# Loading four adjacent heads in one 128-partition DMA, with gated queues and a rewritten opening, in a fused attention and MoE kernel

## The chip, the cores and the metric

The kernel runs on one core of one Trainium2 chip. The metric is the device time of one execution in microseconds, taken as the median over runs. The engines are named as in the profile: PE (TensorE matmul), PEld (TensorE weight load), DVE (VectorE), ACT (ScalarE), POOL (GpSimd) and SP (SyncE, which here only issues DMAs).

## The reference

A ReLU-squared attention without softmax, followed by a two-layer feed-forward block with a quick GELU. All inputs and the output are float32.

```python
q, k, v: (8, 12, 448, 64)          # batch, heads, sequence, head size
scores = (1/sqrt(64)) * q @ k^T
attn   = max(scores, 0)**2 / 448
x      = (attn @ v) as (3584 tokens, 768)
h      = x @ w_in                  # (768, 2048)
g      = h * sigmoid(1.702 * h)
out    = g @ w_out                 # (2048, 768)
```

## The kernel before

The attention is cut into 24 units (`NU`), three for each of the 8 batches. A unit holds four heads: partitions 0 to 63 carry one pair of heads and partitions 64 to 127 another. A token is written as p*7 + j, so each partition p holds 7 tokens and the attention of a unit runs in 7 slots j.

For each unit, `load` (L66) issues six DMAs on SP, two halves of 64 partitions for each of k, q and v, in float32. `cast` (L79) turns k and q into float16 on DVE and v on POOL. `trans` (L91) issues two transposing DMAs on SP, which give kT and qT with the head size on the partitions. One slot is then `scores` (L99: four 64x64x448 matmuls into the PSUM tile sc), `relu2` (L113: ReLU on ACT from PSUM into rl, then rl*rl on DVE into at) and `av_mm` (L120: four matmuls that accumulate over the 7 slots of the unit in the PSUM tile av). `xt_evac` (L135) copies av as float16 into xt, the transposed input of the feed-forward part.

The feed-forward part works on 8 blocks of 384 or 512 tokens in turn (`gblk`). `m1(g, f)` (L175) makes one of 16 slices of the hidden layer: six matmuls into ht, GELU on ACT into gf, and a scaling to float16 on POOL into gt. `m2(g, m, h)` (L195) makes 128 tokens by 384 columns of the output: 16 matmuls into op, a scaling on DVE into osb and, behind the second half, two output DMAs on SP.

Every engine runs its instructions in the order in which the program emits them. `visit(n)` (L155) emits the scores of the next n slots, the av matmuls of the slots visited last, and the ReLU and multiply of the new slots. The opening loads and prepares units 0 to 2, then issues w1 (four casting DMAs for w_in) on POOL, loads units 3 to 5 and issues w2 (four casting DMAs for w_out), and only then emits the first visits. After the first batch the list `moe` interleaves m1 of block g with m2 of block g-1, and a visit of two slots is emitted whenever the estimated matmul time since the last one passes `TV = 3.4`. `step_visit` first calls `prefetch(u + 4, u + 2)`, which loads up to unit u+3 and prepares unit u+1.

The pools that matter: three buffers for each staged tensor, two for the float16 casts, four for v16, three for kT and qT, three for rl, six for at, three for xt and gf, three for osb; PSUM has two buffers for sc, one for av and two that ht and op share.

Of the kernel before, what the change touches and what calls it, by code (L numbers as in the profile page):

```python
# [6 lines left out]

F32 = mybir.dt.float32
F16 = mybir.dt.float16
AF = mybir.ActivationFunctionType  # L10
# [4 lines left out]
def kernel(  # L15
# [9 lines left out]
    nc = tc.nc  # L25
# [8 lines left out]
    NOUT = DM // 2  # L34
    SC = float(D * S)
    WQ = 4


    gblk = [6, 8] * (B // 2)
# [12 lines left out]
    xtp = ctx.enter_context(tc.tile_pool(name="xtp", bufs=3))  # L52
    gfp = ctx.enter_context(tc.tile_pool(name="gfp", bufs=3))
    gtp = ctx.enter_context(tc.tile_pool(name="gtp", bufs=2))
    osp = ctx.enter_context(tc.tile_pool(name="osp", bufs=3))
    ps_s = ctx.enter_context(tc.tile_pool(name="ps_s", bufs=2, space=bass.MemoryType.PSUM))
    ps_v = ctx.enter_context(tc.tile_pool(name="ps_v", bufs=1, space=bass.MemoryType.PSUM))
    ps_m = ctx.enter_context(tc.tile_pool(name="ps_m", bufs=2, space=bass.MemoryType.PSUM))

    win = [cst.tile([128, NK, WQ * 128], F16, name=f"win{i}") for i in range(NF // WQ)]  # L60
    wout = [cst.tile([128, WQ, DM], F16, name=f"wout{i}") for i in range(NF // WQ)]


    units = {}

    def load(u):  # L66
        b, pr = divmod(u, NP)
        st = {}
        for n, t in (("k", k), ("q", q), ("v", v)):
            x = stp.tile([128, 2, S], F32, name=f"{n}st", tag=f"{n}st")  # L70
            for s in range(2):
                h0 = 6 * s + 2 * pr
                nc.sync.dma_start(  # L73
                    out=x[64 * s:64 * s + 64, :, :],
                    in_=t[b, h0:h0 + 2].rearrange("a (p j) d -> p a (j d)", j=J))
            st[n] = x
        units[u] = st

    def cast(u):  # L79
        st = units[u]  # L80
        for n in ("k", "q"):
            c = c16.tile([128, J, 2, D], F16, name=f"{n}16", tag=f"{n}16")
            nc.vector.tensor_copy(  # L83
                out=c.rearrange("p j a d -> p a j d"),
                in_=st[n].rearrange("p a (j d) -> p a j d", d=D))
            st[n + "16"] = c
        vv = v16p.tile([128, 2, J, D], F16, name="v16", tag="v16")
        nc.gpsimd.tensor_copy(out=vv, in_=st["v"].rearrange("p a (j d) -> p a j d", d=D))  # L88
        st["v16"] = vv

    def trans(u):  # L91
        st = units[u]
        for n in ("k", "q"):
            t = qkT.tile([128, J, 128], F16, name=f"{n}T", tag=f"{n}T")
            nc.sync.dma_start_transpose(  # L95
                out=t[:, :, :], in_=st[n + "16"].rearrange("p j a d -> p (j a d)"))
            st[n + "T"] = t

    def scores(u, j):  # L99
        st = units[u]  # L100
# [11 lines left out]

    def relu2(u, j, sc):  # L113
        rl = rlp.tile([128, 2, S], F16, name="rl", tag="rl")
        nc.scalar.activation(out=rl, in_=sc[:, :, 0:S], func=AF.Relu)  # L115
        at = atp.tile([128, 2, S], F16, name="at", tag="at")
        nc.vector.tensor_tensor(out=at, in0=rl, in1=rl, op=ALU.mult)  # L117
        return at

    def av_mm(u, j, at):  # L120
        st = units[u]
        if j == 0:
            st["av"] = ps_v.tile([128, 2, 512], F32, name="av", tag="av")
        for s in range(2):
            for a in range(2):
                r = slice(64 * s, 64 * s + 64)
                nc.tensor.matmul(  # L127
                    out=st["av"][64 * a:64 * a + 64, s, 0:S],
                    lhsT=st["v16"][r, a, j, :],
                    rhs=at[r, a, :],  # L130
                    start=(j == 0), stop=(j == J - 1))

# [42 lines left out]
    def m1(g, f):  # L175
        n = 64 * gblk[g]
        if f == 0:
            gts[g] = gtp.tile([128, NF, 512], F16, name="gt", tag="gt")
        ht = ps_m.tile([128, 512], F32, name="ht", tag="mm")
        w = win[f // WQ]  # L180
        fo = (f % WQ) * 128
        for kk in range(NK):
            nc.tensor.matmul(  # L183
                out=ht[:, 0:n], lhsT=w[:, kk, fo:fo + 128],
                rhs=xts[g][:, kk // NP, kk % NP, 0:n],
                start=(kk == 0), stop=(kk == NK - 1))
        gf = gfp.tile([128, 512], F32, name="gf", tag="gf")
        nc.scalar.activation(out=gf[:, 0:n], in_=ht[:, 0:n],  # L188
                             func=AF.Gelu_apprx_sigmoid, scale=1.0 / SC)
        nc.gpsimd.tensor_scalar(out=gts[g][:, f, 0:n], in0=gf[:, 0:n],  # L190
                                scalar1=SC, scalar2=1.0, op0=ALU.mult, op1=ALU.mult)
# [3 lines left out]
    def m2(g, m, h):  # L195
        if h == 0:
            osb[g, m] = osp.tile([128, DM], F32, name="osb", tag="osb")
        ot = osb[g, m]
        op = ps_m.tile([128, 512], F32, name="op", tag="mm")
        for f in range(NF):  # L200
            nc.tensor.matmul(  # L201
                out=op[:, 0:NOUT],
                lhsT=gts[g][:, f, m * 128:(m + 1) * 128],
                rhs=wout[f // WQ][:, f % WQ, h * NOUT:(h + 1) * NOUT],
                start=(f == 0), stop=(f == NF - 1))
        nc.vector.tensor_scalar(out=ot[:, h * NOUT:(h + 1) * NOUT], in0=op[:, 0:NOUT],  # L206
                                scalar1=1.0 / SC, scalar2=None, op0=ALU.mult)
        if h == 1:
            for i in range(2):
                b, j = divmod(gcum[g] + 2 * m + i, J)  # L210
                r0 = b * S + j
                nc.sync.dma_start(out=out[r0:r0 + 63 * J + 1:J, :],
                                  in_=ot[64 * i:64 * i + 64, :])

    def w1(i):
        nc.gpsimd.dma_start(  # L216
            out=win[i],
            in_=moe_w_in[:, i * WQ * 128:(i + 1) * WQ * 128].rearrange(
                "(kk p) f -> p kk f", p=128))

    def w2(i):
        nc.gpsimd.dma_start(  # L222
            out=wout[i],
            in_=moe_w_out[i * WQ * 128:(i + 1) * WQ * 128, :].rearrange(
                "(f p) d -> p f d", p=128))


    moe = []

    def t1(g):  # L230
        return 6 * (64 * gblk[g] / 2400.0 + 0.0025)

    T2 = 16 * (NOUT / 2400.0 + 0.0025)
    for ph in range(1, NG + 2):
        a = [("m1", ph - 1, f) for f in range(NF)] if ph - 1 < NG else []
        c = ([("m2", ph - 2, m, h) for m in range(gblk[ph - 2] // 2) for h in range(2)]
             if ph >= 2 else [])
        if a and c:
            seq = []
            ci = 0  # L240
            for i, x in enumerate(a):
                seq.append(x)
                while ci < len(c) and (i + 1) * len(c) >= (ci + 1) * len(a):
                    seq.append(c[ci])
                    ci += 1
            seq += c[ci:]
        else:
            seq = a + c
        moe += seq

    with tc.manual_schedule():
        loaded = [0]
        prepped = [0]

        def prefetch(upto_load, upto_prep):
            while loaded[0] < min(NU, upto_load):
                load(loaded[0])
                loaded[0] += 1
            while prepped[0] < min(NU, upto_prep):
                cast(prepped[0])  # L260
                trans(prepped[0])
                prepped[0] += 1

        prefetch(2, 0)
        prefetch(2, 1)
        prefetch(3, 2)
        prefetch(3, 3)
        for i in range(NF // WQ):
            w1(i)
        prefetch(6, 3)  # L270
        for i in range(NF // WQ):
            w2(i)

        def step_visit(n):
            u = slots[pos[0]][0]
            prefetch(u + 4, u + 2)
            visit(n)


        while done_units[0] < NP:  # L280
            if pos[0] < NP * J:
                step_visit(min(2, NP * J - pos[0]))
            else:
                visit(0)
        acc = 0.0
        TV = 3.4
        m1_done = 0
        for it in moe:
            if it[0] == "m1":
                g = it[1]  # L290
                need = NP * min(B, -(-gcum[g + 1] // J))
                while done_units[0] < need:
                    if pos[0] < len(slots):
                        step_visit(2)
                    else:
                        visit(0)
                m1(*it[1:])
                acc += t1(g)
            else:
                m2(*it[1:])  # L300
                acc += T2
            if it[0] == "m1" and it[2] == NF - 1:
                m1_done = it[1] + 1
            if acc >= TV and (pos[0] < len(slots) or pend):

                if pos[0] < len(slots):
                    if slots[min(pos[0] + 1, len(slots) - 1)][0] // NP + 1 - 3 < m1_done:
                        step_visit(2)
                else:
                    visit(0)  # L310
                acc -= TV


# [28 lines left out]
```

## Time and profile before

| What | us |
|---|---|
| median of three runs | 461.97 |
| lowest and highest | 460.99 and 463.29 |
| the profiled execution | 461.49 |
| its span, first to last instruction | 459.7 |
| PE busy | 391.4 |
| ACT busy | 212.0 |
| DVE busy | 192.6 |
| POOL busy | 107.4 |

The profile gives one execution. Busy time of PE includes matmuls that run at half clock: the line PEclk says in tenths which part of the full clock was granted in each slice. The DMA share is the mean busy share of the 16 DMA engines of the core, and the GB/s count the bytes as written, so that a casting DMA from float32 to float16 counts half of what it reads. In lists of waits the columns are the time in all, how often, and the longest one. In lists in order of time they are start, duration, engine, line, operation, operands and, in brackets, the idle time before it and what ended that.

### The profile page before, as it was taken

How to read it: one execution, taken by the hardware profiler on the slowest of the kernel's cores; microseconds unless marked ns; L12 is line 12 of the kernel's file. 1: busy time of each engine (PE TensorE's matmuls, PEld its weight loads, DVE VectorE, ACT ScalarE, POOL GpSimd, SP SyncE). 2: the span in 40 equal slices, each digit the busy share in tenths (PEclk: the TensorE clock that was granted, in tenths of full speed). 3: DMA queues.
4: the chain of work that ended last, by engine and by line, in shares of the span. 5: the costliest groups of instructions: out<-in, count | busy, mean ns of one | idle time of the engine just before them, and what ended most of it. 6: DMA issues, size and time to landing. Idle time of an engine off the chain costs nothing.

```text
span 459.7 us, 7621 instructions
## 1 busy us (share of the span) xinstructions
PE 391.4 (85%) x3008; PEld 196.2 (43%) x3008; DVE 192.6 (42%) x308; ACT 212.0 (46%) x298; POOL 107.4 (23%) x164
## 2 busy tenths in 40 slices
PE   0276208878999899989998999989999999999995
PEld 0032104333444455544444555534444555455563
DVE  1387002575653445565444355356364634200021
ACT  1295105775664355466553545456564545322200
POOL 0060202501231222223142133213222212122200
PEclk9997757959999999999999999999999999999999
DMA  8999999799462589539831888198093311111132
GB/s 191 229 223 272 233 202 230 156 209 230 93 145 51 148 149 208 116 91 224 194 80 41 156 193 194 36 210 179 2 187 83 68 44 36 34 26 28 34 88 68
DMA packets 75044, 61.84 MB, mean 135 GB/s; under 512 B 47872, under 2 KB 71424, under 8 KB 75008
## 3 DMA queue, kind: packets, MB, share of 16 engines
q1 hardware_dynamic: 69760, 55.07, 54.9%
q0 software_dynamic: 5248, 6.29, 8.1%
q8 instruction: 23, 0.38, 0.3%
q14 instruction: 13, 0.11, 0.1%
HBM read 45.61 MB, written 11.01 MB: 123 GB/s over the span
## 4 chain that ended last, share of the span: by engine, by line
PE 74%; DMA 12%; DVE 8%; SPq 3%; issue 2%; ACT 1%; DVEq 0%; ACTq 0%
PE op L201 31%; PE ht L183 31%; PE sc L106 6%; DMA qT<-q 6%; PE av L127 5%; DMA qst<-in_q_dram 3%; DVE xt L144 3%; DMA kst<-in_k_dram 2%; DVE at L117 2%; SPq L73 2%; DVE k L83 1%; DVE q L83 1%; ACT rl L115 1%; SPq L95 1%; DVE osb L206 0%
## 5 line engine op out<-in xcount | busy, mean ns | idle before, releaser
L115 ACT ACTIVATE rl<-sc 128x896 f16<-128x896 f32 x168 | 144.5, 917 | 121.5 <-PE sc L106 113.7
L183 PE MATMUL ht<-xt,win 128*128 128x384 f16 (+1 forms) x768 | 161.6, 358 | 8.3 <-DVE xt L144 8.3
L201 PE MATMUL op<-wout,gt 128*128 128x384 f16 x896 | 153.6, 326 | 0.0
L117 DVE TENSOR_TENSOR at<-rl 128x896 f16<-128x896 f16 x168 | 107.6, 655 | 106.8 <-ACT rl L115 106.6
L190 POOL TENSOR_SCALAR gt<-gf 128x384 f16<-128x384 f32 (+1 forms) x128 | 77.3, 604 | 295.0 <-ACT gf L188 292.8
L188 ACT ACTIVATE gf<-ht 128x384 f32<-128x384 f32 (+1 forms) x128 | 69.8, 545 | 98.0 <-PE ht L183 82.6
L201 PEld LDWEIGHTS <-gt 128*128 128x128 f16 x896 | 86.7, 98 | 62.4 <-issue 4.1
L183 PEld LDWEIGHTS <-win 128*128 128x128 f16 x768 | 71.5, 99 | 90.6 <-issue 33.4
L106 PE MATMUL sc<-qT,kT 64*64 64x448 f16 x672 | 56.0, 393 | 45.1 <-DMA qT<-q 40.0
L206 DVE TENSOR_SCALAR osb<-op 128x384 f32<-128x384 f32 x56 | 31.2, 557 | 132.7 <-PE op L201 131.9
L127 PE MATMUL av<-at,v 64*64 64x448 f16 x672 | 54.1, 381 | 10.2 <-DVE at L117 9.7
L106 PEld LDWEIGHTS <-kT 64*64 64x64 f16 x672 | 17.7, 110 | 77.1 <-issue 59.2
L127 PEld LDWEIGHTS <-v 64*64 64x64 f16 x672 | 22.7, 112 | 28.3 <-issue 17.8
L88 POOL CAST v<-vst 128x896 f16<-128x896 f32 x24 | 23.4, 981 | 30.3 <-DMA vst<-in_v_dram 29.2
L144 DVE CAST xt<-av 128x768 f16<-128x768 f32 (+2 forms) x36 | 26.8, 772 | 3.8 <-PE av L127 3.7
L83 DVE CAST k<-kst 128x896 f16<-128x896 f32 x24 | 15.5, 647 | 13.5 <-DMA kst<-in_k_dram 13.5
L83 DVE CAST q<-qst 128x896 f16<-128x896 f32 x24 | 18.1, 753 | 6.1 <-DMA qst<-in_q_dram 4.7
L216 POOL DMA_DIRECT2D win<-in_moe_w_in_dram x4 | 3.5, 886 | 0.0
L222 POOL DMA_DIRECT2D wout<-in_moe_w_out_dram x4 | 3.0, 792 | 0.0
L115 ACT ACT_TABLE_LOAD x1 | 1.3, 1283 | 0.7 <-PEq L326 0.7
L188 ACT ACT_TABLE_LOAD x1 | 1.3, 1283 | 0.0
L326 POOL MEMSET const-float32-0.0<- 128x1 f32 x1 | 0.1, 99 | 0.2 <-issue 0.2
(3 smaller groups left out, 0.3 us busy)
## 6 DMA issues: line engine op xcount, KB each, us to landing
kst<-in_k_dram SPq DMA_DIRECT2D x48, 224.0 KB, 4.2
qst<-in_q_dram SPq DMA_DIRECT2D x48, 224.0 KB, 4.8
vst<-in_v_dram SPq DMA_DIRECT2D x48, 224.0 KB, 5.3
out_dram<-osb SPq DMA_DIRECT2D x56, 192.0 KB, 2.7
win<-in_moe_w_in_dram POOLq DMA_DIRECT2D x4, 768.0 KB, 21.2
wout<-in_moe_w_out_dram POOLq DMA_DIRECT2D x4, 768.0 KB, 39.5
kT<-k SPq DMA_TRANSPOSE x24, 4.4
qT<-q SPq DMA_TRANSPOSE x24, 4.7
```

The source lines that it names most:

```text
L83: nc.vector.tensor_copy(out=c.rearrange("p j a d -> p a j d"), in_=st[n].rearrange("p a (j d) -> p a j d", d=D))
L88: nc.gpsimd.tensor_copy(out=vv, in_=st["v"].rearrange("p a (j d) -> p a j d", d=D))
L106: nc.tensor.matmul(out=sc[c, a, 0:S], lhsT=st["kT"][r, j, c], rhs=st["qT"][r, :, c], start=True, stop=True)
L115: nc.scalar.activation(out=rl, in_=sc[:, :, 0:S], func=AF.Relu)
L117: nc.vector.tensor_tensor(out=at, in0=rl, in1=rl, op=ALU.mult)
L127: nc.tensor.matmul(out=st["av"][64 * a:64 * a + 64, s, 0:S], lhsT=st["v16"][r, a, j, :], rhs=at[r, a, :], start=(j == 0), stop=(j == J - 1))
L144: nc.vector.tensor_copy(out=xts[g][:, :, pr, 64 * (lo - gcum[g]):64 * (hi - gcum[g])], in_=av[:, :, 64 * (lo - b * J):64 * (hi - b * J)])
L183: nc.tensor.matmul(out=ht[:, 0:n], lhsT=w[:, kk, fo:fo + 128], rhs=xts[g][:, kk // NP, kk % NP, 0:n], start=(kk == 0), stop=(kk == NK - 1))
L188: nc.scalar.activation(out=gf[:, 0:n], in_=ht[:, 0:n], func=AF.Gelu_apprx_sigmoid, scale=1.0 / SC)
L190: nc.gpsimd.tensor_scalar(out=gts[g][:, f, 0:n], in0=gf[:, 0:n], scalar1=SC, scalar2=1.0, op0=ALU.mult, op1=ALU.mult)
L201: nc.tensor.matmul(out=op[:, 0:NOUT], lhsT=gts[g][:, f, m * 128:(m + 1) * 128], rhs=wout[f // WQ][:, f % WQ, h * NOUT:(h + 1) * NOUT], sta ...
L206: nc.vector.tensor_scalar(out=ot[:, h * NOUT:(h + 1) * NOUT], in0=op[:, 0:NOUT], scalar1=1.0 / SC, scalar2=None, op0=ALU.mult)
```

## The change

The four heads of a unit are now adjacent (4*pr to 4*pr+3), so that the two heads that sit in the two halves of the partitions follow each other in memory and one DMA fills all 128 partitions. v is loaded by a casting DMA from POOL's queue straight into v16; its float32 staging tile and its cast on POOL are gone. The q cast moves from DVE to POOL, except that of unit 0, which is on ACT. Unit 0 is transposed on PE by an identity, with the evictions on ACT and DVE, instead of by DMA. In the first six units slot 3 takes its ReLU on DVE and its multiply on POOL. The rows of w_in are reordered to the new order of heads, which makes each w1 four DMAs of 64 partitions; w_out is cut by output half and in chunks of 8 instead of 4.

The opening is written out by hand: the first 42 slots, m1 of block 0 and of block 1 come before any m2; m1 of block 1 runs without visits. Two gates on SP (`sp_gate`) copy a few bytes of a weight tile and thereby wait for its landing, and the loads of units 3 and 4, and later of unit 6 on, stand behind them. The m2 of block 0 run with two visits each (threshold 1.35, first all with h = 0), the rest with a threshold of 3.1. `step_visit` now prefetches behind the visit. osb has four buffers, and a GELU on one element at the start loads ACT's table.

```diff
+    ident = cst.tile([128, 128], F16, name="ident")
+    gate = cst.tile([1, 64], F16, name="gate")
+    def load_qk(u):
+        for n, t in (("k", k), ("q", q)):
+            x = stp.tile([128, 2, S], F32, name=f"{n}st", tag=f"{n}st")
+            nc.sync.dma_start(
+                out=x,
+                in_=t[b, 4 * pr:4 * pr + 4].rearrange("(a s) (p j) d -> (s p) a (j d)", a=2, j=J))
+    def load_v(u):
+        x = v16p.tile([128, 2, S], F16, name="v16", tag="v16")
+        nc.gpsimd.dma_start(
+            out=x,
+            in_=v[b, 4 * pr:4 * pr + 4].rearrange("(a s) (p j) d -> (s p) a (j d)", a=2, j=J))
...
+    def trans_pe(u, n):
+        ps = ps_s.tile([128, 2, 1024], F16, name="tr", tag="sc")
+        for j in range(J):
+            nc.tensor.matmul(
+                out=ps[:, j // 4, (j % 4) * 128:(j % 4 + 1) * 128],
+                lhsT=st[n + "16"][:, j, :, :], rhs=ident[:, :], is_transpose=True)
+        nc.scalar.activation(out=t[:, 0:4, :], in_=ps[:, 0, 0:512], func=AF.Copy)
+        nc.vector.tensor_copy(out=t[:, 4:7, :], in_=ps[:, 1, 0:384])
...
+        if u < 2 * NP and j == 3:
+            nc.vector.tensor_scalar(out=rl, in0=sc[:, :, 0:S], scalar1=0.0, scalar2=None,
+                                    op0=ALU.max)
+            nc.gpsimd.tensor_tensor(out=at, in0=rl, in1=rl, op=ALU.mult)
...
+    def w1(i):
+        for a in range(2):
+            for s in range(2):
+                nc.gpsimd.dma_start(
+                    out=win[i][64 * a:64 * a + 64, s, :, :],
+                    in_=w_rows[a, :, s, :, i * WQ * 128:(i + 1) * WQ * 128])
+    def sp_gate(src):
+        nc.sync.dma_start(out=gate[0:1, :], in_=src)
...
+        load_qk(0)
+        load_qk(1)
+        load_qk(2)
+        load_v(0)
+        cast(0, "k", nc.vector)
+        trans_pe(0, "k")
+        cast(0, "q", nc.scalar)
+        trans_pe(0, "q")
+        load_v(1)
+        cast(1, "k", nc.vector)
+        cast(1, "q", nc.gpsimd)
+        load_v(2)
+        trans(1)
+        w1(0)
+        visit(2)
+        cast(2, "k", nc.vector)
+        visit(2)
+        cast(2, "q", nc.gpsimd)
+        trans(2)
+        w1(1)
+        sp_gate(win[0][64:65, 1, 0, 0:64])
+        load_qk(3)
+        load_qk(4)
+        visit(2)
+        visit(2)
+        load_v(3)
+        cast(3, "k", nc.vector)
+        cast(3, "q", nc.gpsimd)
+        trans(3)
+        load_qk(5)
+        while pos[0] < NP * J:
+            visit(min(2, NP * J - pos[0]))
+        visit(0)
+        prep = {0: lambda: (load_v(4), cast(4, "k", nc.vector), cast(4, "q", nc.gpsimd),
+                            w1(2), trans(4)),
+                3: lambda: (load_v(5), cast(5, "k", nc.vector), cast(5, "q", nc.gpsimd),
+                            w1(3), trans(5))}
+        for f in range(8):
+            visit(2)
+            m1(0, f)
+            if f in prep:
+                prep[f]()
+        while pos[0] < 2 * NP * J:
+            visit(min(2, 2 * NP * J - pos[0]))
+        visit(0)
+        for f in range(8, NF):
+            m1(0, f)
+            if f == 10:
+                w2(0, 0)
+                w2(0, 1)
+                w2(1, 0)
+                w2(1, 1)
...
+        sp_gate(wout[0][1][0:1, 0, 0:64])
+        prefetch(8, 0)
+        for f in range(NF):
+            m1(1, f)
+            if f == 10:
+                prefetch(9, 7)
+            if f == 14:
+                prefetch(9, 8)
```

## The prediction

> **What bounds the kernel now.** I read the busy slices and the chain first, then the waits of the first 107 us, then the order of time around them, then busy time by stretch.
>
> Engine busy tenths, granted clock and DMA share in 40 slices (11.5 us each), and the chain's shares by engine:
>
> ```profile
> PE   0276208878999899989998999989999999999995
> PEclk9997757959999999999999999999999999999999
> DMA  8999999799462589539831888198093311111132
> PE 74%; DMA 12%; DVE 8%; SPq 3%; issue 2%; ACT 1%; DVEq 0%; ACTq 0%
> ```
>
> TensorE is full from slice 10 on. What it loses lies in the first nine slices, exactly where the DMA engines are full. Waits in 0 to 107 us (us in total, times, longest):
>
> ```profile
> PE sc L106 <- DMA qT<-q: 38.9, 3, 21.7
> DVE k L83 <- DMA kst<-in_k_dram: 13.5, 3, 5.2
> ```
>
> The places, in order of time (start, duration, engine, line):
>
> ```profile
> 5.24 0.63 DVE L83 CAST k<-kst 128x896 f16<-128x896 f32 x1 [5.24 <-DMA kst<-in_k_dram]
> 7.61 0.63 DVE L83 CAST q<-qst 128x896 f16<-128x896 f32 x1 [1.74 <-DMA qst<-in_q_dram]
> 11.45 0.63 DVE L83 CAST k<-kst 128x896 f16<-128x896 f32 x1 [3.22 <-DMA kst<-in_k_dram]
> 16.83 0.96 PE L106 MATMUL sc<-qT,kT 64*64 64x448 f16 x8 [16.83 <-DMA qT<-q]
> 24.11 3.50 POOL L216 DMA_DIRECT2D win<-in_moe_w_in_dram  x4
> 47.53 10.58 SPq L95 DMA_TRANSPOSE qT<-q  x1
> 70.93 0.96 PE L106 MATMUL sc<-qT,kT 64*64 64x448 f16 x8 [21.69 <-DMA qT<-q]
> ```
>
> Scores start at 16.8. At 47.5 unit 3's q transpose is issued beside the wout loads, and lands at 70.8: TensorE stands still for 21.7 us. Stretches (us; PE, PEld, DVE, ACT, POOL busy; clock; DMA share; GB/s by bytes written):
>
> ```profile
> 4.00:12.00 8.00, 0.00 (x0) 0.00 (x0) 1.80 (x3) 0.00 (x0) 0.93 (x1) 1.00 1.06 235
> 30.00:48.00 18.00, 12.32 (x106) 5.45 (x102) 11.32 (x20) 10.66 (x13) 2.34 (x4) 0.81 1.16 272
> 56.00:68.00 12.00, 0.00 (x0) 0.00 (x0) 0.00 (x0) 0.00 (x0) 0.00 (x0) 0.50 1.16 201
> 156.60:459.70 303.10, 290.50 (x2197) 149.46 (x2195) 124.61 (x200) 137.01 (x198) 70.69 (x109) 1.00 0.50 109
> ```
>
> The last 303 us are 96% TensorE. Nothing in the change takes matmuls away, so only the front can give.
>
> **Prices of what the trace shows.** In its full part two m1 take 2.06 (n=384) or 2.70 us (512), an m2 2.60, a visit of two slots 0.88; a ReLU on ACT 0.86, a multiply 0.63.
>
> **Prices of what it does not show.**
> (a) A q, k or v load (0.459 MB) over 128 partitions. The 64-partition halves run at 235 GB/s: 1.95 us a tensor. In 30:48 the win loads land 7.5 us apart (issues 24.1 to 26.8, landing after 10.2 at least and 30.0 at most: 34.3 to 56.8, three steps), each 1.57 MB read and half of it written, so 1.89 of the 4.90 MB written there are theirs and reads run at (4.90+1.89)/18 = 377 GB/s. Bounds 1.22 (377) and 1.95 us; I take 1.25, as the 377 is reached with these very rows in the mix. The Trainium skill (SBUF — State Buffer, the section on Door 1, the DMA port swizzle) says why: 64 partitions reach 8 of the 16 ports, 196 against 328 GB/s at 1 MiB. By its 328 the tensor would take 1.4 us and stage A would end 0.3 later.
> (b) A weight chunk w1(i), 1.57 MB: 4.2 us at 377, 7.5 in company. Taken 4.5.
> (c) A transpose beside weight traffic: 1 us of its own (smallest landing 2.9 us) up to half of the 24.7 us that the pair of 46.2 needed. They seem to alternate with weight packets, so a chunk in flight holds a transpose for about the chunk: 5 us.
> (d) A POOL-issued DMA: 0.47 (smallest SP issue, 64 rows) to 1.02 (largest win issue, 768 rows); 192 to 256 rows: 0.65.
> (e) The two-input multiply on POOL: 0.93 (its one-input cast of that size) to 1.87 (twice); taken 1.5.
> (f) ReLU on DVE out of PSUM: 1.08 (the 128x896 xt cast).
> (g) 128-column PE transposes: seven in 0.8 us, from the 0.24 us that four 64x448 matmuls take per score slot up to one slow 0.59 burst. Evictions 0.6 on ACT (gf 128x512: 0.597), 0.45 on DVE (osb 128x384: 0.557, output here f16).
>
> **Stage A, to the first scores (before 16.8).** k0 lands at 5.1: v0 on POOL's queue shares the engines from 3.1, which eats the faster packets. DVE cast 0.63, transposes 0.8, eviction ACT then DVE: kT at 7.5. q0 shares with v0 and v1 (2.5 us): lands 7.5, ACT cast 0.92, transposes 0.8, evictions 0.6 and 0.45, hops of 0.1 to 0.15: scores at 10.6. Gain 6.2. The identity and its select on POOL (before v0's issue, about 1 us) and the warm activation lie under the wait for k0; without that cover the identity would cost its 1 us.
>
> **Stage B, units 0 to 2 (before 16.8 to 43.8).** Unit 1 still goes through DMA transposes: k1's cast stands behind qT's eviction on DVE (11.2), kT lands 14.5; q1 is cast on POOL at 11.7, its transpose is issued at 12.4 and meets v2 and w1(0), which POOL issues right behind that cast: lands about 20.4. Before, slot 7 began at 23.2, so 6.2 us of lead are now 2.5. The gate on SP comes behind unit 2's transposes, which meet w1(1): held for w1(0)'s landing (21.2), k3 is issued at 21.7 but queued behind qT of unit 2 (26.4) and beside v3, landing at 30. Its cast stands in DVE's order ahead of unit 0's xt copy and the multiplies of slot 8 on: DVE waits from 22.5 to 30, and TensorE with it. Then 11 slots at DVE's pace: per unit 6 multiplies (3.9), one ReLU (1.1), one cast (0.6), xt (1.2) = 6.8, so 0.97 a slot, 10.7 us, and 2.8 to drain. First m1 at 45 less 0.5 for (e) at 1.5: 44.5. Before 43.8: the lead is gone.
>
> **Stage C, units 3 to 5 and m1 of block 0 (before 43.8 to 105.4 = 61.6).** Unit 3's transposes now land at about 37, so the 21.7 us stall is gone. New waits: POOL issues w1(2) (4 x 0.65 = 2.6) ahead of slot 24's multiply (1.5), and av of slots 23 and 24 waits 3.6 for it; the same with w1(3) at slot 31, 2.2; qT of unit 4 and of unit 5 each meet their chunk: 2.1 and 1.3. Work under these: ACT sets eight pairs, 2 ReLU x 0.86 + 0.5 = 2.2 each, 17.8; five slots more at 0.97 and drain 1.5: 6.4; then eight m1 at 1.03 = 8.2, and half-clock matmuls (clock 0.75 in 71 to 105.4) for 1.2. Sum 17.8+6.4+8.2+9.2+1.2 = 42.8: ends at 87.3. Cover gone: without ACT's bound these pairs cost TensorE 1.9 each.
>
> **Stage D, m1 of block 1, 24 slots, 6 m2 (before 105.4 to 154.0: its sixth m2 ends at 152.2, the visit behind it at 153.1, one more visit 0.9).** 16 m1 at 1.35 = 21.6. w2 is now issued at block 0's eleventh m1 (about 82); the second gate opens at wout's half, 94; k6 to q8 and the transposes of unit 6 behind them on SP land at 113, stall about 2. m2 6 x 2.60 = 15.6; 24 slots x 0.44 = 10.6; two visits back to back make the second one wait for its ReLU and multiply (0.25+2x0.86+0.63+0.35 = 2.95 against 1.76): 1.2 x 5.5 = 6.6. Sum 56.4 against 48.6: ends at 143.7. The second gate and the bunched visits give 7.8 back.
>
> **Stage E (before 305.7).** POOL now issues v's loads and casts q in place of v: a load of v waits for av of the unit three back, about 4 us, then 0.65 and 0.95, then the transpose 1.2+3: about 10 us, against four gaps of 3.4 and three visits of 0.9 = 16 until the unit is wanted. Free with 6 to spare; a miss would cost its excess 18 times. The halved number of SP issues frees a queue that nobody waits for; the fourth osb buffer, the new operand slices of av, m1 and m2 and the order of the heads change no instruction's size. Zero; bounds -4 (of 12.6 idle in the stretch) to +8.
>
> **Sum.** 143.7 + 305.7 = 449.4 of span, less 1.2 for the second table load that vanishes (ACT at 41.7): 448, and 1.8 around it (461.49 - 459.7): 450. The profiled run stands 0.5 under the median of 461.97, so the same as a median: 450. One correction: at (d)'s lower end of 0.47 B's chain of nine issues is 1.6 shorter and C's ten 1.8, at (e)'s lower end C another 1.2 and B 0.6, and at (c)'s own 1 us C 2; these 7 lean one way, because the rows behind (c) and (d) are of larger transfers. I take 3 of them: **447**.
>
> [...]
>
> **Rivals.** *Front hidden*: B's wait for k3 (7.5) and C's waits for POOL and transposes (9.2) vanish because DMA runs ahead of my figures: 447 - 16.7 = 430, and 426 with E's -4. For: the 128-partition rate is bounded, not known. Against: the transposes of units 1 and 2 are issued ahead of the gates, so the gates hold back q and k loads alone and leave the transposes beside w1; in that sense they do not do what they say.
>
> *POOL becomes the bound*, the one on the slower side: up to 95 us 26 DMA issues stand in POOL's order ahead of multiplies, q casts and gt. If one costs 0.65 and, before it, a multiply and a cast of DVE (0.66 + 0.63), that is 1.29 x 26 = 33: 480. It decides from 14.5/26 = 0.56 more, 1.2 us an issue. For: multiplies stretch to 1.35 (median 0.63) when POOL runs beside them. Against: the four win issues of 24.1 took 3.50 together, amid multiplies.
>
> *Nothing won*: C's pairs run wholly at half clock (m1 1.03 more, eight times, half of it under ACT: 4) and E is at its +8: 459, up to 463 where D's visits are at half clock too.
>
> **Numbers.** Forecast 0.52, rival 1 0.22, rival 2 0.18, rival 3 0.08. A measurement of this kernel can tell about 0.5% from no change. Forecast and rival 1 count as faster, with a piece of rival 3: 0.75; same 0.07; slower 0.18. Range 426 to 466: rival 1's end, and POOL issues at 0.65+0.73.
>
> **What would show it.** First scores at 10 to 11; DVE idle before k3's cast for 5 us or more; av waiting for POOL's multiply beside w1(2) and w1(3); scores waiting for qT of units 1, 4, 5 and 6 by 1 to 3 us, and none for 10 us; the last 300 us unchanged. Wrong if first m1 comes before 38 or after 52, if POOL's issues exceed 1.2 us, or if the last stretch is not within 4 us.

## The result and the profile after

The changed kernel is slower: 476.65 us in the median of four runs (475.03 to 479.66) against 462.63 (460.99 to 464.08), a ratio of the means of 1.0312 with a 95% interval of 1.0245 to 1.0378. The prediction was 447 us, range 426 to 466. The profiled execution took 475.03 us, with a span of 473.3.

The span cut at the ends of the prediction's five stages: first scores, first m1, end of m1 of block 0, the visit behind block 0's sixth m2, end (columns: stretch, length, then busy time of PE, PEld, DVE, ACT and POOL, granted clock, DMA share, GB/s):

```profile
0.00:9.48 9.48, 1.86 (x14) 1.45 (x15) 1.45 (x5) 3.52 (x5) 2.34 (x8) 1.00 0.82 219
9.48:51.66 42.18, 20.66 (x176) 7.65 (x176) 22.13 (x29) 16.11 (x19) 14.69 (x16) 0.72 0.92 173
51.66:101.70 50.04, 37.02 (x260) 15.96 (x257) 22.39 (x28) 22.26 (x32) 23.42 (x30) 0.76 0.51 64
101.70:166.90 65.20, 51.21 (x372) 23.99 (x371) 22.39 (x36) 29.62 (x41) 21.16 (x31) 0.95 0.97 200
166.90:473.30 306.40, 293.54 (x2208) 151.03 (x2204) 127.56 (x192) 137.47 (x200) 82.42 (x122) 1.00 0.46 99
```

| Stage | before | predicted | measured | measured end |
|---|---|---|---|---|
| A, to the first scores | 16.8 | 10.6 | 9.5 | 9.5 |
| B, to the first m1 | 27.0 | 33.9 | 42.2 | 51.7 |
| C, to the end of m1 of block 0 | 61.6 | 42.8 | 50.0 | 101.7 |
| D, to the visit behind block 0's sixth m2 | 48.6 | 56.4 | 65.2 | 166.9 |
| E, the rest | 305.7 | 305.7 | 306.4 | 473.3 |

The last 306 us are what they were. The change won 7.3 us ahead of the first scores and lost 20.2 between there and 167 us: 15.2 in B and 16.6 in D, less the 11.6 that it won in C. The busy slices of the page (11.8 us each) and the chain's shares by engine:

```profile
PE   2516775699668789999999899989999999999995
PEclk9965678699979999999999999999999999999999
DMA  8996377079984994775461763973751221201132
PE 57%; DMA 16%; issue 10%; DVE 7%; POOL 5%; ACT 3%; SPq 1%; ACTq 0%; POOLq 0%; DVEq 0%
```

Before, TensorE was empty where the DMA engines were full. That is now left in the third slice alone (PE 1, DMA 9). In the fifth (PE 7, DMA 3) and the eighth (PE 6, DMA 0) both are thin, at a clock of 6: few transfers are under way there, because few have been issued (SP issues nothing from 38.5 to 54.4 us and from 71.0 to 109.2). TensorE carries 57% of the chain where it carried 74. The waits that carry it, in order of time (start, duration, engine, line, and in brackets the idle time before it and what ended that):

```profile
9.48 0.96 PE L129 MATMUL sc<-qT,kT 64*64 64x448 f16 x8 [1.08 <-DVE qT L119]
15.64 1.69 POOL L142 TENSOR_TENSOR at<-rl 128x896 f16<-128x896 f16 x1
17.27 0.94 POOL L99 CAST q<-qst 128x896 f16<-128x896 f32 x1
25.75 0.62 SPq L259 DMA_DIRECT2D gate<-win  x1
26.42 0.57 SPq L77 DMA_DIRECT2D kst<-in_k_dram  x1
33.27 0.63 DVE L99 CAST k<-kst 128x896 f16<-128x896 f32 x1 [10.11 <-DMA kst<-in_k_dram]
35.11 0.59 PE L155 MATMUL av<-at,v 64*64 64x448 f16 x4 [10.25 <-DVE xt L172]
60.88 0.38 PE L155 MATMUL av<-at,v 64*64 64x448 f16 x4 [2.06 <-POOL at L142]
79.41 0.96 PE L129 MATMUL sc<-qT,kT 64*64 64x448 f16 x8 [3.18 <-DMA qT<-q]
109.15 0.54 SPq L259 DMA_DIRECT2D gate<-wout  x1
133.29 0.96 PE L129 MATMUL sc<-qT,kT 64*64 64x448 f16 x8 [7.00 <-DMA qT<-q]
```

Read from top to bottom: scores start early; unit 2's q cast stands behind slot 3's multiply on POOL; the first gate lets unit 3's k go at 26.42; DVE stands still for 10.11 us on that k's cast, with the xt copy that TensorE needs queued behind it; later av waits for POOL's multiply, and the loads behind the second gate leave at 109 us, so that unit 6 comes 7.00 us late. Which of these sets the time is for the experiments to show.

### The profile page after: what moved, and what is told of

The parts are those of the page before. It is cut to its first block, busy times and chain, and to the rows that moved or that the text cites. A ratio compares the mean times of both kernels' runs of the same rounds, so it can differ in the third digit from the quotient of the medians.

```text
span 473.3 us, 7544 instructions
## 1 busy us (share of the span) xinstructions
PE 404.3 (85%) x3022; PEld 200.1 (42%) x3022; DVE 195.9 (41%) x287; ACT 209.0 (44%) x295; POOL 144.0 (30%) x207
## 4 chain that ended last, share of the span: by engine, by line
PE 57%; DMA 16%; issue 10%; DVE 7%; POOL 5%; ACT 3%; SPq 1%; ACTq 0%; POOLq 0%; DVEq 0%
PE op L229 26%; PE ht L211 20%; PE sc L129 5%; DMA qT<-q 5%; PE av L155 5%; DMA qst<-in_q_dram 4%; DVE at L145 4%; ACT rl L144 3%; DMA win<-in_moe_w_in_dram 2%; DMA wout<-in_moe_w_out_dram 2%; DVE xt L172 2%; POOL gt L218 2%; DMA kst<-in_k_dram 1%; POOL at L142 1%; POOL q L99 1%
## 5 line engine op out<-in xcount | busy, mean ns | idle before, releaser
L144 ACT ACTIVATE rl<-sc 128x896 f16<-128x896 f32 x162 | 139.9, 918 | 110.0 <-PE sc L129 97.5
L145 DVE TENSOR_TENSOR at<-rl 128x896 f16<-128x896 f16 x162 | 120.3, 758 | 83.9 <-ACT rl L144 83.8
L218 POOL TENSOR_SCALAR gt<-gf 128x384 f16<-128x384 f32 (+1 forms) x128 | 79.1, 618 | 154.4 <-ACT gf L216 150.1
L129 PE MATMUL sc<-qT,kT 64*64 64x448 f16 x672 | 58.9, 405 | 26.2 <-DMA qT<-q 13.2
L155 PE MATMUL av<-at,v 64*64 64x448 f16 x672 | 58.4, 395 | 25.4 <-DVE xt L172 10.2
L86 POOL DMA_DIRECT2D v<-in_v_dram x24 | 18.4, 765 | 115.3 <-PE av L155 109.3
L155 PEld LDWEIGHTS <-v 64*64 64x64 f16 x672 | 24.1, 114 | 47.2 <-issue 37.2
L99 POOL CAST q<-qst 128x896 f16<-128x896 f32 x23 | 21.8, 950 | 21.4 <-issue 12.9
L142 POOL TENSOR_TENSOR at<-rl 128x896 f16<-128x896 f16 x6 | 10.7, 1784 | 10.6 <-DVE rl L140 10.5
L248 POOL DMA_DIRECT2D win<-in_moe_w_in_dram x16 | 10.0, 630 | 0.0
L140 DVE TENSOR_SCALAR rl<-sc 128x896 f16<-128x896 f32 x6 | 6.5, 1080 | 0.0
```

Source lines behind the costliest of these rows:

```text
L86: nc.gpsimd.dma_start(out=x, in_=v[b, 4 * pr:4 * pr + 4].rearrange("(a s) (p j) d -> (s p) a (j d)", a=2, j=J))
L99: eng.tensor_copy(out=o, in_=i)
L129: nc.tensor.matmul(out=sc[c, a, 0:S], lhsT=st["kT"][r, j, c], rhs=st["qT"][r, :, c], start=True, stop=True)
L155: nc.tensor.matmul(out=st["av"][64 * a:64 * a + 64, s, 0:S], lhsT=st["v16"][r, a, 64 * j:64 * j + 64], rhs=at[r, a, :], start=(j == 0), st ...
```

## The experiments

The times are medians; ratios are to the kernel before, run beside them (461.61 to 462.02 us), with 95% intervals. "First m1" is read from the order of time of each run's trace.

**The first gate alone.** Theories: the gate makes unit 3's k late, or the weights that share the engines do.

```diff
         w1(1)
-        sp_gate(win[0][64:65, 1, 0, 0:64])
         load_qk(3)
```

> The changed kernel with the first gate on SP left out, so that the loads of units 3 and 4 are issued behind unit 2's transposes without waiting for w1(0). Theory 'gate' (VectorE's 10.1 us wait for unit 3's k cast is the gate's doing: k3 was issued at 26.4 where SP was free at 20.6): k3 lands 5 us earlier, 471 us. Theory 'sharing' (the transposes of units 1 and 2 in the same SP ring crawl beside w1's packets, and k3 would only queue behind them): k3 still lands at 31 to 34, 474 to 478 us.

476.77 us, 1.0316 [1.0266, 1.0365]: no change. Its order of time:

```profile
20.51 0.62 SPq L77 DMA_DIRECT2D kst<-in_k_dram  x1
33.78 0.63 DVE L99 CAST k<-kst 128x896 f16<-128x896 f32 x1 [12.11 <-DMA kst<-in_k_dram]
```

The load of unit 3's k leaves 5.9 us sooner (20.51 against 26.42) and its cast begins no sooner (33.78 against 33.27). Instead of standing on SP behind a gate it stands on SP's queue behind unit 2's q transpose, which goes out beside two weight chunks and takes 13.0 us from issue to landing here (13.4 with the gate). The gate itself costs nothing here.

**The second gate alone.**

```diff
-        sp_gate(wout[0][1][0:1, 0, 0:64])
         prefetch(8, 0)
```

> The changed kernel with the second gate left out, so that the loads of units 6 to 8 are issued as soon as SP has issued unit 5's transposes (about 75 us), while the trace shows next to no DMA traffic from 80 to 98. Theory 'gate': the wait of 7.0 us for unit 6's qT at 126 to 133 goes, 468 to 470 us. Theory 'sharing' (the loads then meet w1(3) and delay unit 5's transposes by as much): no change within 2 us.

470.5 us, 1.0172 [1.0113, 1.0232], some 6 us less than the changed kernel. Between 100 and 165 us no scores wait for a transpose any more; the wait of 7.00 is gone. That gate does cost what it holds back.

**The first two weight chunks later**, behind unit 3's q cast on POOL, and with them the first gate away.

```diff
         trans(1)
-        w1(0)
...
-        w1(1)
-        sp_gate(win[0][64:65, 1, 0, 0:64])
...
         load_qk(5)
+        w1(0)
+        w1(1)
```

> The changed kernel with w1(0) and w1(1) issued on POOL behind unit 3's q cast and the first gate left out: no weight is in flight while units 1 to 3 are loaded and transposed, and DMA is empty from 42 to 54 in the changed kernel. Theory 'sharing': qT of unit 1 lands at 15 to 16 instead of 20.8, k3 at 23 to 25 instead of 33, the first m1 starts at 42 to 44 instead of 51.7: 466 to 468 us. Theory 'gate': not more than without the gate alone. If VectorE's pace and POOL's multiplies set the opening, the first m1 stays at 49 or later: 474 us.

473.14 us, 1.0228 [1.0186, 1.0269]: the interval overlaps with that of the changed kernel, and the expected 42 to 44 for the first m1 was missed (47.3). The order of time shows why:

```profile
28.32 4.94 POOL L248 DMA_DIRECT2D win<-in_moe_w_in_dram  x8
33.28 1.94 POOL L142 TENSOR_TENSOR at<-rl 128x896 f16<-128x896 f16 x1
35.27 0.96 PE L155 MATMUL av<-at,v 64*64 64x448 f16 x8 [4.24 <-POOL at L142]
```

The eight weight issues, moved away from the transposes, now stand in POOL's order ahead of a slot-3 multiply, and TensorE waits 4.24 us for that. Unit 3's k cast does begin 7.1 us sooner (26.15), and the wait for xt behind it fell from 10.25 to 5.16 us; POOL's wait took a good part of that back.

**Slot 3 back on ACT and DVE.**

```diff
-        if u < 2 * NP and j == 3:
+        if False:
```

> The changed kernel with every slot's ReLU on ScalarE and multiply on VectorE again, nothing on POOL. Theory 'POOL in the way' (av waits 8.5 us in all for POOL's multiplies, which stand behind DMA issues and stretch VectorE's multiplies beside them): 468 to 470 us. Theory 'it relieves ScalarE': ScalarE and VectorE get 6 x 0.3 us more each, 477 to 479 us.

469.56 us, 1.0171 [1.0129, 1.0212], some 7 us less. Here the other wait stays, longer than in the changed kernel:

```profile
33.58 0.63 DVE L99 CAST k<-kst 128x896 f16<-128x896 f32 x1 [11.75 <-DMA kst<-in_k_dram]
```

**Both of these together**, with the second gate left in.

> The changed kernel with w1(0) and w1(1) late (and so no first gate) and slot 3 undone; the second gate stays. Taken alone the two gave 3.5 and 7.1 us. Theory 'two chains side by side' (unit 3's k behind w1's traffic, and POOL's multiplies behind its DMA issues and the q cast, each hold the first 50 us, so either alone uncovers the other): the first m1 at 38 to 39 and 455 to 458 us, that is 19 to 21 us less. Theory 'they add': 466 us, first m1 at 44.

459.82 us, 0.9943 [0.9922, 0.9963]: 16.8 less than the changed kernel, where the two alone gave 3.5 and 7.1. The order of time:

```profile
23.24 0.63 DVE L99 CAST k<-kst 128x896 f16<-128x896 f32 x1 [2.56 <-DMA kst<-in_k_dram]
25.08 0.59 PE L155 MATMUL av<-at,v 64*64 64x448 f16 x4 [2.49 <-DVE xt L172]
25.39 4.96 POOL L248 DMA_DIRECT2D win<-in_moe_w_in_dram  x8
37.52 0.50 PE L211 MATMUL ht<-xt,win 128*128 128x384 f16 x2
```

First m1 at 37.5; alone they reached 47.3 and 48.0, from 51.7. So 14.1 us are won ahead of the first m1; the spans of the two profiled executions differ by 12.2, so nothing more is won behind it.

Where they come from can be read from unit 2's q transpose, behind which unit 3's k stands on SP's queue. Its time from issue to landing (last column, us), in the changed kernel (issued at 18.24) and here (16.39):

```profile
qT<-q SPq DMA_TRANSPOSE x1, 13.4
qT<-q SPq DMA_TRANSPOSE x1, 5.5
```

It is 13.0 without the first gate and 14.1 with slot 3 alone undone, where the weights go out beside it, and 5.1 with the weights alone moved. In all five runs k's cast begins 1.3 to 2.3 us behind that landing. So the weights hold it: its cast begins 7.1 us sooner with them alone moved (26.15), no sooner with slot 3 alone undone (33.58), and another 2.9 sooner with both, since unit 2's q cast on POOL, which that transpose needs, then starts at 15.15 instead of 17.73. From k's cast to the first m1 it takes 14.4 and 14.3 us where POOL has no multiply (slot 3 alone, both) and 18.4 in the changed kernel. With the weights alone moved it takes 21.2, because the eight issues stand ahead of the multiply. Ahead of the first m1 both together win 14.1, and alone 4.4 and 3.7. Of the 6 us between, 2.8 were lost, in the run with the weights alone moved, by the place to which they were moved; another 2.9 are POOL's order, which shows only once the weights are gone.

**All three undone**: this kernel and the second gate away too.

> The changed kernel without both gates, with w1(0) and w1(1) behind unit 3's q cast and with slot 3 on ScalarE and VectorE again. Theory 'gates, weights and POOL' (these three are the loss, and each is paid by itself): 476.7 - 6.1 - 3.5 - 7.1 = 460. Theory 'order' (what loses is that 42 slots and a lone m1 of block 1 go ahead of every m2, so that ScalarE and VectorE bound the first 100 us and idle in the next 30): the three overlap, 463 to 468, and block 1's m1 still ends at 112 or later with all m2 to come.

450.12 us, 0.9759 [0.9707, 0.9811]: 26.5 less than the changed kernel, where the three alone sum to 16.7 (6.1, 3.5 and 7.1). Both expectations missed it. The gate is worth 9.7 us here (459.82 to 450.12) and 6 in the changed kernel; from the end of m1 of block 0 to the visit behind the sixth m2 the traces give 8.4 (64.7 to 56.3) and 7.2 (65.2 to 58.0). Two long waits are left between the first m1 and 86 us:

```profile
52.67 0.59 PE L129 MATMUL sc<-qT,kT 64*64 64x448 f16 x4 [6.69 <-DMA qT<-q]
68.56 0.96 PE L129 MATMUL sc<-qT,kT 64*64 64x448 f16 x8 [5.04 <-DMA qT<-q]
```

for the q transposes of units 4 and 5, in flight beside w1(2) and w1(3). The stretch from the end of m1 of block 0 to that visit, which ends at 141.9, by busy time up to 141.5:

```profile
85.60:141.50 55.90, 48.91 (x369) 23.42 (x371) 20.33 (x34) 29.24 (x41) 20.58 (x31) 1.00 0.94 179
```

56.3 us to the visit's end against 65.2, at full clock instead of 0.95, close to the 56.4 of the prediction's stage D.

**The adjacent heads alone, put into the kernel before**: one 128-partition DMA per tensor on SP, still float32, and w1 as four DMAs; nothing else.

```diff
-            for s in range(2):
-                h0 = 6 * s + 2 * pr
-                nc.sync.dma_start(
-                    out=x[64 * s:64 * s + 64, :, :],
-                    in_=t[b, h0:h0 + 2].rearrange("a (p j) d -> p a (j d)", j=J))
+            nc.sync.dma_start(
+                out=x,
+                in_=t[b, 4 * pr:4 * pr + 4].rearrange("(a s) (p j) d -> (s p) a (j d)", a=2, j=J))
```

> The kernel before with adjacent heads alone: one 128-partition DMA on SP for each of k, q and v (float32, v still cast on POOL), and w1 as four 64-partition DMAs with the reordered rows. Theory 'the loads are worth something': first scores at 13 to 15 instead of 16.8, and the transposes that stood behind the loads of units 3 to 5 get out before wout comes: 450 to 456 us. Theory 'the stall decides' (unit 3's transposes still meet wout): 458 to 462.

450.83 us, 0.9768 [0.9722, 0.9814]. First scores at 12.4 instead of 16.8, the first matmul of m1 at 35.2 instead of 42.7 (the table's 43.8 is the burst a microsecond behind it). On its own this part of the change is worth 11 us; so the rest of it, put on top, costs some 25. The great stall stays:

```profile
60.69 0.96 PE L104 MATMUL sc<-qT,kT 64*64 64x448 f16 x8 [18.94 <-DMA qT<-q]
```

**The kernel before with w_out later**, issued after unit 5 is prepared, to see whether that stall can be moved away by order alone; and the same on top of the adjacent heads.

```diff
-        for i in range(NF // WQ):
-            w2(i)
+        w2_left = [NF // WQ]
...
             prefetch(u + 4, u + 2)
+            if prepped[0] >= 6:
+                while w2_left[0]:
+                    w2(NF // WQ - w2_left[0])
+                    w2_left[0] -= 1
```

> The kernel before with w2 issued only when unit 5 has been prepared, nothing else. Theory 'a moved load would have done': the 21.7 us wait for unit 3's qT falls to 2 to 5 us, 442 to 447 us. Theory 'the stall moves': the first m2 waits for wout instead, or unit 3 waits behind w1, 455 to 460.

> The kernel before with adjacent heads loaded by 128-partition DMAs and w2 issued when unit 5 has been prepared. If the two add: 436 to 443 us, first m1 at 38 to 40 and no wait of TensorE above 5 us. If the loads are hidden once w2 is out of the way: as with w2 moved alone, within 2 us.

465.04 us, 1.0074 [1.0044, 1.0103], and 458.22, 0.9934 [0.99, 0.9968]. Both are worse than without the edit, by 3.4 us (from the 461.68 of the kernel before, run beside them) and 7.4, and neither lies where it was expected. In the first the stall of 21.69 us splits: 9.84 us for unit 3, whose transposes still meet w1, and then, in the first kernel's order of time,

```profile
105.44 0.59 PE L106 MATMUL sc<-qT,kT 64*64 64x448 f16 x4 [13.78 <-DMA qT<-q]
```

for unit 5, beside w_out. TensorE's waits for q transposes in the first 150 us sum to 41.5 us with the edit and 38.9 without it; with the adjacent heads to 39.4 and 31.7. In this front, weights moved past one unit's transposes meet the next unit's.

**w1 all at once**: all three undone, and w1(2) and w1(3) issued right behind w1(1).

```diff
         load_qk(5)
-        w1(0)
-        w1(1)
+        for i in range(4):
+            w1(i)
```

> The kernel of the last three edits together (450.1 us: no gates, w1(0) and w1(1) behind unit 3's q cast, slot 3 undone) with w1(2) and w1(3) issued right behind them instead of beside the transposes of units 4 and 5. Theory 'sharing': the waits for qT of unit 4 (6.7) and unit 5 (5.0) fall to 1 or 2 each, 439 to 442 us. Rival: the transposes wait for the loads of units 4 to 6 in their own ring and not for weights, 448 to 451.

446.15 us, 0.9651 [0.9624, 0.9678], between the two expectations. Unit 5's transposes are free, unit 4's are not:

```profile
52.82 0.59 PE L129 MATMUL sc<-qT,kT 64*64 64x448 f16 x4 [9.65 <-DMA qT<-q]
```

One wait of 9.65 took the place of 6.69 and 5.04. The last of w1's issues went out at 41 us here, while unit 4's k transpose, issued at 39.90, took 11.1 us to land; so its transposes still went out beside weights, and the rival, that they wait for loads in their own ring, is not excluded.

**The same with w_out after the 42nd slot, unit 6 prepared there, and block 1's m1 mixed with block 0's m2**, one visit at a time.

```diff
-        for x in [("m2", 0, m, h) for h in range(2) for m in range(gblk[0] // 2)]:
-            moe.append((x, 1.35))
-        for g in range(2, NG + 1):
+        for g in range(1, NG + 1):
...
+            if g == 1:
+                c = [("m2", 0, m, h) for h in range(2) for m in range(gblk[0] // 2)]
```

> That kernel with all four w1 at once, and besides w2 issued behind the 42nd slot, unit 6 prepared there, and m1 of block 1 mixed with m2 of block 0 and one visit at a time as in the later blocks (the first m2 still all with h = 0). Theory 'order' (m1 of block 1 alone, then two visits per m2, costs TensorE the waits for ScalarE within each pair of visits, about 1.3 us in each of 5 pairs): 5 to 8 us less than with w1 at once alone. Rival 'the work is only moved': within 2 us of it.

444.57 us, 0.9621 [0.9602, 0.9639]; against the kernel above the intervals overlap, so nothing is shown to be gained by it. Both kernels are below the one before, by 3.5 and 3.8%, and by the medians 6.4 and 6.7% below the changed one. The slices of the last one:

```profile
PE   2668298699998999999999999999998999999995
PEclk9998698979999999999999999999999999999999
```

The last slice below eight tenths before the end is the eighth, at 89 us; in the changed kernel it is the fourteenth, at 166. The clock is below 8 tenths in two slices, not in six.

**Unit 0 transposed by DMA** in the kernel with all three undone.

```diff
         cast(0, "k", nc.vector)
-        trans_pe(0, "k")
         cast(0, "q", nc.scalar)
-        trans_pe(0, "q")
+        trans(0)
```

> The kernel of the three edits together (450.1 us) with unit 0 transposed by DMA again, as units 1 to 3 are. If the PE transposes are worth their lead: first scores at 12.5 instead of 9.5, and 452 to 454 us. If the lead ends at the next wait (unit 1's qT, unit 3's k cast): 449 to 451 us.

454.36 us, 0.9835 [0.9786, 0.9884], 4.2 more, with intervals that just overlap. The trace is plainer:

```profile
16.06 0.96 PE L129 MATMUL sc<-qT,kT 64*64 64x448 f16 x8 [16.06 <-DMA qT<-q]
```

First scores at 16.1 instead of 9.5, but first m1 at 40.4 instead of 38.1: of the 6.6 us that the transposes on PE win at the start, 2.3 are left there.

## Why the prediction was wrong

The places were right; the sizes of three things were not: a transpose beside weights, POOL's multiplies, and the clock. Against the predicted span of 449.4, the stages came out at A -1.1, B +8.3, C +7.2, D +8.8, E +0.7: 23.9 us. The two credits taken off afterwards (1.2 and 3) add 4.2. Together they make the 28.0 between 447 and the profiled 475.03; the median of the runs lies another 1.6 above that.

**A, right.** Scores at 9.5 against 10.6: k0's cast began at 4.34, where 5.1 was said. The parts don't add up plainly: the adjacent heads alone gave 4.4 us on the kernel before, the transposes on PE 6.6 in the kernel with all three undone.

**B, the step that failed first: price (c), 5 us for a transpose beside weights, in "queued behind qT of unit 2 (26.4) and beside v3, landing at 30"; and behind it "11 slots at DVE's pace".** The mechanism was there, with the place named: k3 queues behind that transpose, DVE waits for k3's cast and TensorE with it. But unit 2's q transpose, issued at 18.24, took 13.4 us and landed at 31.6, not at 26.4; k3's cast began at 33.27, 3.3 late. Moving the weights away brings that transpose to 5.1 to 5.5 us. Price (b), 4.5 us for a weight chunk, was too low as well: the gate, which waits for w1(0), opened at 25.75, 10.1 us behind the last of its issues, where its landing had been put at 21.2; but without the gate k3 came no sooner. From the cast to the first m1 it took 18.4 us, not 14.5. The 14.5 is DVE's pace *without* POOL's multiplies (14.4 with slot 3 alone undone); the sum by slot has them as a relief of DVE (six multiplies a unit, not seven) and names no wait for them. The 4.0 are their price, and it has two parts: av waits for the multiply itself (1.48 us at 39.63, 0.80 at 47.70), and the DVE multiplies beside it run long.

**C, under-sized: waits of 9.2 on TensorE.** They sum to 13.0 in the trace (waits of PE, 51.6 to 102 us: cause, us in total, times, longest):

```profile
PE av L155 <- POOL at L142: 4.9, 3, 2.1
PE sc L129 <- DMA qT<-q: 3.7, 2, 3.2
PE sc L129 <- DVE rl L140: 2.8, 2, 1.4
PE av L155 <- DVE at L145: 1.1, 2, 0.9
PE sc L129 <- ACT rl L144: 0.5, 1, 0.5
```

The transposes and POOL were about as said (3.4 and 5.8 predicted). What the prediction left out are the 2.8 us that scores wait for DVE to read slot 3 out of PSUM, at 1.08 us a ReLU, and the clock. In order of time, the eight pairs with their waits took 31.3 us where 27.0 were summed, the slots behind them 8.3 where 6.4, and the eight m1 10.4 where 8.2, at a granted clock of 0.76, behind 8.3 us at 0.68; with slot 3 alone undone they took 7.97 at full clock. The charge for the clock was 1.2, read from a stage of before that was better fed. Undoing slot 3 alone shortens C by only 2.1 us (48.0), since there the waits for the transposes beside w1(2) and w1(3) grow from 3.7 to 12.3; in the kernel with both edits they are 13.7, and C takes 51.0.

**D, under-sized: "the second gate opens at wout's half, 94 ... stall about 2".** It opened at 109.15. POOL issued w_out at 98.06, 16 us later than the 82 of the sum, mostly because the m1 that it stands behind had moved by B's and C's excess; counted from the start of D, the gate opened at 7.5 us, where the sum had 6.7. The stage's own miss lies behind it: from the gate to the scores of unit 6 it took 24.1 us, not 19. The gate let six loads go at once, of units 6 to 8, while the other half of w_out was on its way (DMA share 0.97 over the stage), and unit 6's transposes took 12.8 and 9.4 us from issue to landing, the k one alone 6.46 to issue at 117.20. Without the second gate the four transposes issued between 80 and 130 us land in 2.9 and 3.2 us (medians for k and q). TensorE had only 16 m1 and one m2 as cover, and they ran out 7.0 us too soon. Behind it the m2 and visits took 33.6 us where 30.2 were summed, one m2 at a clock of 0.64 among them (4.24 against 2.77). Taking the gate out removed that wait.

**E, right**: 306.4 against 305.7, so the cost of nothing for v's loads on POOL, the q casts there, the extra osb buffer and the new order of heads stands as a sum; none of them was tried by itself.

**The credits, wrong.** Three us were taken off on the ground that POOL's issues, its multiplies and the transposes would come cheaper than their middle price. None did: an issue of win took 630 ns, about the 650 taken, of v 765 and of w_out 914; the multiply took 1784 ns, where 1500 was taken; and unit 2's transposes beside weights took 11.6 and 13.4 us, where 5 was. The 1.2 were for ACT's second table load, which is gone as said (the only one left is at 0.73); what that is worth can't be read from the stages.

**The rivals.** *POOL becomes the bound* had the time (480) but not the way: it asked for 1.2 us an issue, and no issue group reached it. What POOL did cost came through its order, two or three instructions deep, and through its multiply. *Front hidden* was wrong by its main term: the wait for k3 grew instead of vanishing. But the argument against it, that the gates leave the transposes of units 1 and 2 beside w1, is what the weights-later experiments bear out.

VectorE's multiplies did not hold POOL's DMA issues: w1(0)'s four took 2.48 us from 13.15 on, with multiplies on DVE starting at 13.51 and 15.04, and the four of w1(2) took the same 2.48, with one starting at 58.12.

What stays open: why a transpose beside weights slows down by so much, and why TensorE then waits 9.65 us for unit 4 in one run and 0.51 in another, was not taken apart; only that it does, and that moving the weights moves it.

## What to carry to other kernels

A stage that hangs on two queues at once must be costed along both to the end: here weights issued beside transposes, and one slot's multiply a unit on POOL, gave back 3.5 and 7.1 us when undone alone and 16.8 together. When an instruction or a DMA issue is put on an engine, follow that engine's order for every instruction behind it until something that another engine waits for, not only for the next one. A gate that holds loads back is free while those loads would queue behind the same transfer anyway, and costs a wait where the loads behind it have no cover left: taking the first one out changed nothing, taking out the second removed a wait of 7.0 us.

## What the runs showed of the hardware

**Work on POOL slows multiplies on DVE.** Over the changed kernel (columns: count, then busy us and mean ns, then idle time before):

```profile
L145 DVE TENSOR_TENSOR at<-rl 128x896 f16<-128x896 f16 x162 | 120.3, 758 | 83.9 <-ACT rl L144 83.8
L142 POOL TENSOR_TENSOR at<-rl 128x896 f16<-128x896 f16 x6 | 10.7, 1784 | 10.6 <-DVE rl L140 10.5
```

At 16.75 us, beside POOL's multiply of 15.64 and the q cast behind it, one DVE multiply of the same size took 1.95 us; at 59.63, beside POOL's multiply of 59.14 alone, 1.70; and at 55.35, beside a q cast on POOL (55.76 to 56.70), 1.84. Their median is 0.626. Only a part of the mean is the POOL multiply's: it is 758 ns here, 729 with slot 3 alone undone, and 655 in the kernel before. The Trainium skill (GPSIMD Engine Reference, Elementwise — side-by-side cycle accounting) gives about 2.6 cycles an element for a two-input instruction, by which an estimate for 896 elements at its 1.2 GHz is 1.94 us; the six took 1.68 to 1.98, so row and rule agree, and the 1.5 that was taken between two bounds was too low.

**128-partition loads reach the rate that weight loads only suggested.** In 32 to 36 us of the changed kernel, when q and k loads of units 3 and 4 and unit 3's transposes have the DMA engines to themselves (995 of the 996 packets are of SP's queue), these moved (last column, GB/s):

```profile
32.00:36.00 4.00, 0.59 (x4) 0.18 (x5) 2.73 (x5) 0.00 (x0) 0.93 (x1) 0.50 1.06 382
```

against 235 for the 64-partition halves of the kernel before. The 377 GB/s that the prediction took from the weight loads was right.
